# First batch of a fused attention kernel: queries loaded in two halves, and the third key tile pooled by TensorE

## The chip, the cores and the metric

The kernel runs on one core of a Trainium2 chip. The metric is device time in microseconds of one execution; the number compared is the median of several executions. A profile of one more execution comes with it: it gives a span (first to last instruction) and, for every engine, what ran when. The engines are TensorE (PE; its weight loads are listed apart as PEld), VectorE (DVE), ScalarE (ACT), GpSimd (POOL) and SyncE (SP), which here only issues transfers. Every engine runs its instructions in the order in which they were written; they meet by semaphores.

## The reference

Two stages follow each other, for a batch of 4, with 12288 queries of 128 channels each and 384 x 32 key pixels of 128 channels:

```python
r = 4
kv_pool = kv.reshape(B, H // r, r, W // r, r, C).mean(axis=(2, 4))
kv_flat = kv_pool.reshape(B, -1, C) @ w_sr
k = v = kv_flat
s = scale * (q @ k.transpose(0, 2, 1))      # softmax over 768 keys
a = np.exp(s - s.max(-1, keepdims=True)); a /= a.sum(-1, keepdims=True) + 1e-09
x = a @ v
# mixture of adapters: 8 experts of rank 16, the two largest logits of x @ w_gate per token
logits = x @ w_gate
out = x + sum over the two experts e of w[e] * ((x @ A[e]) @ B[e])
```

The part that matters here is the first line: every key is the mean of a 4 x 4 block of pixels, that is, a sum over four rows and four columns (the 1/16 is put into w_sr).

## The kernel before, in words

The keys of a batch come in three tiles (NT = 3) of 256 pooled keys. A tile is held as [128, 4, 2, 512] fp32: 128 partitions, the four pixel rows d, two halves u, and four columns of 128 channels. Each row d is one transfer of 512 KB (load_row, L87). The queries are worked through in 96 chunks of 512; a chunk needs three sets of scores, scores(c, r), one for each key tile r: two products into one of two score banks in PSUM (L318) and one exponential on ScalarE (L319) out of it. Two calls of weigh(c, h) then multiply by the values (L330), twelve products each: h = 0 takes the first three blocks of 128 keys, h = 1 the other three. After that come the adapters.

From chunk 2 on, a software loop (for c in range(2, NCH - 1)) interleaves the scores of later chunks with weigh, normalising and the adapters of earlier ones, and GpSimd pools the keys of the next batch. Before it stands the opening, written out by hand, which this change is about.

Opening, transfers. SP issues the rows of tile 0, then 1 MB of queries (chunks 0 to 3, q0, L125), then tiles 1 and 2, then the next queries (L129, L102). Transfers land in about that order.

Opening, VectorE. For each of the three tiles it adds rows 1, 2 and 3 to row 0 (sum_row, L185), and then folds four columns to two and two to one (sum_cols, L189 and L190).

Opening, TensorE and ScalarE. warm() multiplies constants and has no result that is used. tile_keys(t) turns the pooled tile by a product with the identity in transposing mode (L226); its result is copied to kp_keep by ScalarE (L229), for tile 2 by VectorE (L231); w_sr is applied (k_ps, L234) and copied to the keys kfT (L236, or L238 on VectorE). tile_values(t) makes the values of the same tile (v_ps, L244) and copies them to vext. queries(k, bank) turns chunk k's 512 queries (four products, L582) and ScalarE copies them to qT (L585). The order on TensorE is

```python
tile_keys(0, lambda: queries(0, x_bank())); queries(1, x_bank())
scores(0, 0); tile_values(0); queries(2, x_bank())
scores(1, 0); queries(3, x_bank()); scores(2, 0); scores(3, 0)
warm(6); tile_keys(1); warm(2); scores(0, 1); tile_values(1); scores(1, 1)
weigh(0, 0)
tile_keys(2, during)      # during: cast_half(0); scores(2, 1)
cast_half(1); turn_q(2); turn_q(3)
scores(3, 1); scores(0, 2); tile_values(2); scores(1, 2)
weigh(0, 1); next_scores(); normalise(0)
```

cast_half (VectorE, L607) and cast_q (GpSimd, L107) make fp16 copies of later queries; turn_q (SP, L117) is a transposing transfer of them.

Of the kernel before, what the change touches and what calls it, by code (L numbers as in the profile page):

```python
# [10 lines left out]
FP32 = mybir.dt.float32  # L11
# [10 lines left out]
def kernel(  # L22
# [10 lines left out]
    nc = tc.nc  # L33
    P = 128
    B, N, C = q.tensor.shape
# [5 lines left out]
    NTOK = 512  # L41
    NS = NTOK // P
# [16 lines left out]
    ps_t = ctx.enter_context(tc.tile_pool(name="ps_t", bufs=1, space=bass.MemoryType.PSUM))  # L59
    ps_h = ctx.enter_context(tc.tile_pool(name="ps_h", bufs=1, space=bass.MemoryType.PSUM))  # L60
    x_banks = ExitStack()
    ps_x = x_banks.enter_context(tc.tile_pool(
        name="ps_x", bufs=1, side="right", space=bass.MemoryType.PSUM))
# [5 lines left out]
    def mtile(shape, dtype=FP32, name="hd"):  # L69
        return ps_h.tile(shape, dtype, tag="hd", name=name)  # L70

    mm = nc.tensor.matmul
    g_h = qdram.tile([NCH // 2, E, NS, P, 2], F16, name="g_h")
    qflat = q.rearrange("b n c -> (b n) c")
# [5 lines left out]
    kvt = {}  # L80
    NT = NJ // 2
# [7 lines left out]
    def load_kv(b, t):  # L89
        for d in range(4):  # L90
            load_row(b, t, d)

    GROWS = 2048

    HROWS = GROWS // 2
# [19 lines left out]
    def turn_q(i):  # L115
        new_qT(i)
        nc.sync.dma_start(qT[i], q16[i], transpose=True)  # L117

    q01 = kvpool.tile([P, 2, GROWS // NTOK, NS, C], FP32, tag="kvt", name="q01")
    q0, q1 = q01[:, 0], q01[:, 1]  # L120
    for t in range(NT):
        load_kv(0, t)
        if t == 0:

            nc.sync.dma_start(q0, qflat[0:GROWS].rearrange("(k p s) c -> p k s c", p=P, s=NS))  # L125

    def load_half(i):
        q32[i] = q1[:, 2 * i - 4:2 * i - 2].rearrange("p k s c -> p k (s c)")
# [16 lines left out]
    id_f32 = const.tile([P, P], FP32)  # L145
# [25 lines left out]
    kpT, kfT, vext, sqsum = {}, {}, {}, {}  # L171
# [11 lines left out]
    def sum_row(b, t, d, eng):  # L183
        v = kvt[b, t]
        eng.tensor_tensor(v[:, 0], v[:, 0], v[:, d], op=ALU.add)  # L185

    def sum_cols(b, t, eng):
        v = kvt[b, t][:, 0]
        eng.tensor_tensor(v[:, :, 0:2 * C], v[:, :, 0:2 * C], v[:, :, 2 * C:4 * C], op=ALU.add)  # L189
        eng.tensor_tensor(v[:, :, 0:C], v[:, :, 0:C], v[:, :, C:2 * C], op=ALU.add)  # L190

    def stile(name):
        return ps_s.tile([P, 2, NTOK], FP32, tag="sg", name=name)
# [27 lines left out]
    def tile_keys(t, between=lambda: None):  # L221

        k = slice(2 * t * P, 2 * (t + 1) * P)
        kp_ps = ps_t.tile([P, 2 * P], FP32, tag="tp", name="kp_ps")
        for u in range(2):
            mm(kp_ps[:, u * P:(u + 1) * P], kvt[0, t][:, 0, u, 0:C], id_f32, is_transpose=True,  # L226
               start=(u == 0), stop=(u == 1), skip_group_check=True)
        if t < NT - 1:
            nc.scalar.activation(kpT[0][:, k], kp_ps, AF.Copy)  # L229
        else:  # L230
            nc.vector.tensor_copy(kpT[0][:, k], kp_ps)  # L231
        between()
        k_ps = mtile([P, 2 * P], name="k_ps")
        mm(k_ps, w_sr_sb, kpT[0][:, k], start=True, stop=True)  # L234
        if t < NT - 1:
            nc.scalar.activation(kfT[0][:, k], k_ps, AF.Copy)  # L236
        else:
            nc.vector.tensor_copy(kfT[0][:, k], k_ps)  # L238

    def tile_values(t):  # L240
        v_ps = mtile([P, 2, C + E], name="v_ps")
        for g in range(2):
            j = 2 * t + g
            mm(v_ps[:, g], kpT[0][:, j * P:(j + 1) * P], wext, start=(g == 0), stop=(g == 1),  # L244
               skip_group_check=True)
        if t < NT - 1:
            nc.scalar.activation(vext[0][:, 2 * t:2 * t + 2, 0:C + E], v_ps, AF.Copy)
        else:
            nc.vector.tensor_copy(vext[0][:, 2 * t:2 * t + 2, 0:C + E], v_ps)
# [42 lines left out]
    def prep(c):  # L292
        for b, t, d in loads.get(c, ()):
            load_row(b, t, d)
        for b, t, d in sums.get(c, ()):
            sum_row(b, t, d, nc.gpsimd)
            if d == 3:
                sum_cols(b, t, nc.gpsimd)
# [11 lines left out]
    def scores(c, r):  # L310
        b = c // CPB
        if r == 0:
            tt[c] = ttpool.tile([P, NJ, NTOK], F16, tag="tt", name="tt")
        qc = qT[c // 2][:, c % 2 * NS:(c % 2 + 1) * NS].rearrange("p s t -> p (s t)")
        sg = stile("sg")
        for k in range(2):
            j = 2 * r + k
            mm(sg[:, k], kfT[b][:, j * P:(j + 1) * P], qc, start=True, stop=True)  # L318
        nc.scalar.activation(tt[c][:, 2 * r:2 * r + 2], sg, AF.Exp, bias=0.0, scale=scale)  # L319

    def weigh(c, h, banks=None):
        b = c // CPB
        if banks is not None:
            xps[c] = banks
        elif h == 0:
            xps[c] = ps_x.tile([P, 2, 512], FP32, tag="x", name="xps")
        for j in range(h * NH, (h + 1) * NH):
            for s in range(NS):
                o = xps[c][:, s // 2, (s % 2) * VW:(s % 2 + 1) * VW]
                mm(o, tt[c][:, j, s * P:(s + 1) * P], vext[b][:, j, 0:VW],  # L330
                   start=(j == 0 and s % 2 == 0), stop=(j == NJ - 1 and s % 2 == 1),
                   skip_group_check=True)
# [246 lines left out]
    def queries(k, t):  # L579

        for i in range(NS):
            mm(t[:, i * P:(i + 1) * P], q0[:, k, i], id_f32, is_transpose=True,  # L582
               start=(i == 0), stop=(i == NS - 1), skip_group_check=True)
        qt = qT[k // 2][:, k % 2 * NS:(k % 2 + 1) * NS].rearrange("p s t -> p (s t)")
        nc.scalar.activation(qt, t, AF.Copy)  # L585

    def x_bank():
        return ps_x.tile([P, NTOK], FP32, tag="x", name="q_ps")

    def t_bank():  # L590
        return ps_t.tile([P, NTOK], FP32, tag="tp", name="t_ps")
# [1 line left out]
    def warm(count):  # L593

        t = mtile([P, NS, P], name="w_ps")
        for i in range(count):
            mm(t, id_bf, id_bf.unsqueeze(1).broadcast_to([P, NS, P]), start=True, stop=True)
# [8 lines left out]
    def cast_half(k):  # L606
        nc.vector.tensor_copy(q16[2][:, k * NTOK:(k + 1) * NTOK], q32[2][:, k])  # L607

    for t in range(NT):
        for d in range(1, 4):  # L610
            sum_row(0, t, d, nc.vector)
        sum_cols(0, t, nc.vector)
        if t == 0:
            nc.vector.tensor_copy(a_bf.rearrange("p (r e) -> p e r", e=E),
                                  a_f.rearrange("p (e r) -> p e r", e=E))
            nc.vector.tensor_scalar(b_half, b_f, 0.5, None, op0=ALU.mult)
            nc.vector.tensor_copy(b_bf, b_half)
# [3 lines left out]
    def next_scores():  # L621
        if todo:
            scores(*todo.pop(0))

    tile_keys(0, lambda: queries(0, x_bank()))
    queries(1, x_bank())
    scores(0, 0)
    tile_values(0)
    queries(2, x_bank())
    scores(1, 0)  # L630
    queries(3, x_bank())
    scores(2, 0)
    scores(3, 0)
    warm(6)
    tile_keys(1)
    warm(2)
    scores(0, 1)
    tile_values(1)
    scores(1, 1)
    weigh(0, 0)  # L640

    def during():
        cast_half(0)
        scores(2, 1)

    tile_keys(2, during)
    cast_half(1)
    turn_q(2)
    turn_q(3)
    scores(3, 1)  # L650
    scores(0, 2)
    tile_values(2)
    scores(1, 2)
# [21 lines left out]
    for c in range(2, NCH - 1):  # L675
        b, k = divmod(c, CPB)
# [67 lines left out]
        name="ps_e", bufs=1, reuse_waits="tile", space=bass.MemoryType.PSUM))  # L744
# [65 lines left out]
    def tops4(c, top, y):  # L810
# [20 lines left out]
        name="ps_f", bufs=1, side="right", space=bass.MemoryType.PSUM))  # L831
# [73 lines left out]
    with tc.If(bad_v != 0):  # L905
# [11 lines left out]
        with tc.For_i(0, B) as b:  # L917
            nc.sync.dma_start(kp, kp_all[bass.ds(b, 1)].rearrange("o p k -> p (o k)"))
            for h in range(2):
                s = slice(h * NKV // 2, (h + 1) * NKV // 2)  # L920
# [3 lines left out]
            for h in range(2):  # L924
                v_ps = mtile([P, NJ // 2, C + E], name="gv_ps")
                for g in range(NJ // 2):
                    j = h * NJ // 2 + g
                    mm(v_ps[:, g], kp[:, j * P:(j + 1) * P], wext,
                       start=(g == 0), stop=(g == NJ // 2 - 1))
                nc.vector.tensor_copy(v32[:, h * NJ // 2:(h + 1) * NJ // 2], v_ps)  # L930
            with tc.For_i(0, N, P) as t:
# [3 lines left out]
                q_ps = mtile([P, P], name="gq_ps")  # L935
# [4 lines left out]
                for h in range(2):  # L940
                    mm(s_ps[:, h, 0:NKV // 2], qTf, k32[:, h * NKV // 2:(h + 1) * NKV // 2],
                       start=True, stop=True)
# [9 lines left out]
                for h in range(2):  # L952
                    e_ps = mtile([P, NJ // 2, P], name="ge_ps")
                    for g in range(NJ // 2):
                        j = h * NJ // 2 + g
                        mm(e_ps[:, g], e[:, j * P:(j + 1) * P], id_f32, is_transpose=True,
                           start=(g == 0), stop=(g == NJ // 2 - 1))
# [4 lines left out]
                x = g_w[:, 2, 0:C + E]  # L962
# [63 lines left out]
```

## Time and profile before

| | us |
|---|---|
| median of 3 runs | 379.06 (378.99, 381.55, 379.06) |
| the profiled execution | 378.6 |
| its span | 376.8 |
| TensorE busy | 359.5 |
| ScalarE busy | 310.1 |
| VectorE busy | 300.4 |
| GpSimd busy | 225.1 |

In rows of the timeline and of the chain, the first two numbers are the start and the duration in us from the start of the span; a group of instructions (x8) has the time from its first start to its last end. What stands in square brackets is how long the engine was idle before it, and what ended the wait. A row of the table by stretches gives the stretch and its length, then for PE, PEld, DVE, ACT and POOL the busy time and the number of instructions, then the granted clock of TensorE, the share of the transfer engines and GB/s. A fp32 product that is not a transposing one appears as two matmul rows.

### The profile page before, as it was taken

The numbers are of one execution on the slowest core, as the hardware profiler recorded it, in microseconds if no ns is written. First come the engines' busy times: TensorE is split into PE (matmuls) and PEld (weight loads), VectorE is DVE, ScalarE is ACT, GpSimd is POOL, SyncE is SP. The second block draws the span as 40 slices with busy tenths as digits, with TensorE's granted clock in tenths as the row PEclk, the third lists the DMA queues.
The fourth block names the chain that finished last, engine by engine and source line by source line (L and its number), as shares of the span: only waits on it lengthen the run. The fifth ranks groups of instructions, "written<-read, shape, count | busy, mean of one in ns | idle before, by whom it ended". The sixth has DMA issues, their size and how long they took to land.

```text
span 376.8 us, 10584 instructions
## 1 busy us (share of the span) xinstructions
PE 359.5 (95%) x3943; PEld 265.0 (70%) x3943; DVE 300.4 (80%) x950; ACT 310.1 (82%) x391; POOL 225.1 (60%) x375
## 2 busy tenths in 40 slices
PE   4889999999999999999999999999999999999983
PEld 1446767777777677777777777777776767776772
DVE  3784557888888788788888888888888898889983
ACT  1569999898898898988988898898888888888752
POOL 1013799979699887755679687755434234242244
PEclk9999999999999999999999999999999999999998
DMA  8998999999999999999999999998788699654325
GB/s 260 402 363 202 307 295 331 319 285 303 286 341 318 273 293 328 232 312 317 301 294 370 289 313 308 234 305 262 235 221 259 201 257 242 184 141 142 115 85 198
DMA packets 95593, 101.00 MB, mean 268 GB/s; under 512 B 58804, under 2 KB 59060, under 8 KB 95540
## 3 DMA queue, kind: packets, MB, share of 16 engines
q1 hardware_dynamic: 94068, 100.11, 94.5%
q8 instruction: 31, 0.51, 0.6%
q10 hardware_dynamic: 1472, 0.20, 0.3%
q14 instruction: 22, 0.18, 0.2%
HBM read 62.33 MB, written 25.90 MB: 234 GB/s over the span
## 4 chain that ended last, share of the span: by engine, by line
PE 78%; DVE 7%; POOL 7%; DMA 4%; issue 1%; ACT 1%; ACTq 0%; SPq 0%; POOLq 0%; DVEq 0%
PE xps L330 32%; PE sg L318 28%; PE d_ps L478 5%; PE t_ps L397 5%; PE h_ps L432 4%; DMA b_f<-in_moe_B_dram 3%; POOL kvt L185 2%; DMA kvt<-in_kv_dram 2%; DVE xn L341 2%; DVE ht L435 1%; PE v_ps L209 1%; DVE kvt L185 1%; POOL q L107 1%; POOL kvt L189 1%; PE kp_ps L201 1%
## 5 line engine op out<-in xcount | busy, mean ns | idle before, releaser
L319 ACT ACTIVATE tt<-sg 128x1024 f16<-128x1024 f32 x288 | 277.6, 1022 | 37.9 <-PE sg L318 37.0
L318 PE MATMUL sg<-qT,kfT 128*128 128x512 f16 x576 | 170.1, 379 | 0.4 <-ACT qT L585 0.3
L330 PEld LDWEIGHTS <-tt 128*128 128x128 f16 x2304 | 147.7, 98 | 28.5 <-DVE xn L341 18.6
L330 PE MATMUL xps<-vext,tt 128*128 128x137 f16 x2256 | 166.5, 223 | 0.3 <-DVE xn L341 0.2
L492 DVE TENSOR_TENSOR osb<-d_ps,xn 128x512 f32<-128x512 f32 x85 | 58.7, 691 | 30.0 <-PE d_ps L478 29.7
L357 POOL TENSOR_TENSOR arg<-xn,top 128x64 f32<-128x64 f32 x47 | 14.7, 313 | 102.0 <-DVE top L348 86.2
L341 DVE TENSOR_TENSOR xn<-xps,rinv_all 128x548 f32<-128x548 f32 x94 | 68.4, 728 | 3.3
L318 PEld LDWEIGHTS <-kfT 128*128 128x128 f16 x576 | 49.2, 98 | 24.1 <-issue 0.6
L185 POOL TENSOR_TENSOR kvt<-kvt 128x1024 f32<-128x1024 f32 x27 | 63.6, 2357 | 2.6 <-PE sg L318 2.5
L107 POOL CAST q<-q 128x1024 f16<-128x1024 f32 x45 | 46.8, 1041 | 24.8 <-DMA q<-in_q_dram 24.6
L435 DVE SCALAR_TENSOR_TENSOR ht<-ge,h_ps 128x512 bf16<-128x512 f16 x87 | 58.5, 672 | 1.5 <-PE sg L318 1.0
L478 PEld LDWEIGHTS <-ht 128*128 128x128 bf16 x368 | 27.3, 97 | 24.9 <-DVE ht L435 4.5
L348 DVE MAX8 top<-xn 128x8 f32<-128x8 f32 x376 | 35.1, 156 | 6.2
L408 DVE COPY xt<-t_ps 128x512 bf16<-128x512 bf16 x92 | 36.7, 399 | 0.0
L397 PE MATMUL t_ps<-id_bf,xn 128*128 128x128 bf16 x376 | 36.3, 219 | 0.0
L478 PE MATMUL d_ps<-b_bf,ht 128*128 128x128 bf16 x340 | 32.9, 219 | 1.0 <-DVE ht L435 0.9
L432 PE MATMUL h_ps<-xt,a_bf 128*128 128x512 bf16 x87 | 33.0, 379 | 0.1
L337 DVE RECIPROCAL rinv_all<-xps 128x4 f32<-128x4 f32 x94 | 17.1, 182 | 14.6 <-PE xps L330 12.3
L397 PEld LDWEIGHTS <-xn 128*128 128x128 bf16 x376 | 25.9, 98 | 0.3
L360 POOL TENSOR_SCALAR msk<-msk 128x64 f32<-128x64 f32 x47 | 20.1, 428 | 4.1
L361 POOL TENSOR_TENSOR arg<-arg,msk 128x64 f32<-128x64 f32 x47 | 15.0, 319 | 3.9
L359 POOL TENSOR_TENSOR arg<-arg,msk 128x64 f32<-128x64 f32 x47 | 15.0, 319 | 3.7
(147 smaller groups left out, 220.8 us busy)
## 6 DMA issues: line engine op xcount, KB each, us to landing
kvt<-in_kv_dram SPq DMA_DIRECT2D x48, 512.0 KB
q<-in_q_dram SPq DMA_DIRECT2D x46, 512.0 KB
out_dram<-osb SPq DMA_DIRECT2D x44, 512.0 KB
ge<-g_h SPq DMA_DIRECT2D x45, 256.0 KB
out_dram<-osb SPq DMA_DIRECT2D x8, 256.0 KB
q<-in_q_dram SPq DMA_DIRECT2D x1, 1024.0 KB
qT<-q SPq DMA_TRANSPOSE x46
g_h<-g_sb SPq DMA_DIRECT2D x45, 16.0 KB
```

The source lines that it names most:

```text
L107: nc.gpsimd.tensor_copy(q16[i], q32[i].rearrange("p k n -> p (k n)"))
L185: eng.tensor_tensor(v[:, 0], v[:, 0], v[:, d], op=ALU.add)
L318: mm(sg[:, k], kfT[b][:, j * P:(j + 1) * P], qc, start=True, stop=True)
L319: nc.scalar.activation(tt[c][:, 2 * r:2 * r + 2], sg, AF.Exp, bias=0.0, scale=scale)
L330: mm(o, tt[c][:, j, s * P:(s + 1) * P], vext[b][:, j, 0:VW], start=(j == 0 and s % 2 == 0), stop=(j == NJ - 1 and s % 2 == 1), skip_group_ ...
L341: nc.vector.tensor_tensor(xn[c].rearrange("p (b s) v -> p b s v", b=2), xv, ri.rearrange("p (b s) -> p b s", b=2).unsqueeze(3).broadcast_t ...
L397: mm(columns(t_ps, c, s), src[:, s], id_bf, is_transpose=True, start=(s == 0), stop=(s == NS - 1), skip_group_check=True)
L408: nc.vector.tensor_copy(to, t_ps)
L432: mm(h_ps, a_bf, xT[c], start=True, stop=True)
L435: nc.vector.scalar_tensor_tensor(hgT[c].rearrange("p (k a) t -> p k (a t)", k=2), gE[c // 2][:, h:h + NS // 2].rearrange("p a t k -> p k ( ...
L478: mm(dps[c][:, s], columns(hgT[c], c, s), b_bf, start=(s == 0 and fresh), stop=(s == NS - 1), skip_group_check=True)
L492: nc.vector.tensor_tensor(osb[:, lo:hi], d, xn[c][:, lo:hi, 0:C], op=ALU.add)
```

## The change

The 1 MB of queries becomes two transfers of 512 KB: chunks 0 and 1 behind tile 0, chunks 2 and 3 behind tile 1. In tile 2 VectorE no longer adds rows; it folds the columns of rows 1, 2 and 3, each by itself. TensorE adds the rows: turn_row(d, u) multiplies by the identity, now as ordinary fp32 products, and accumulates all rows in PSUM. Row 0 is not folded at all; its four columns are four products. So there are fourteen such products in place of two transposing ones. They use the second half of a two-bank tile x_all, whose first half holds the queries being turned. queries(2) and queries(3), weigh(0, 0), scores(2, 1) and scores(3, 1) change places, and the warm-up products after the first 18 go from eight to four.

```diff
-        if t == 0:
-
-            nc.sync.dma_start(q0, qflat[0:GROWS].rearrange("(k p s) c -> p k s c", p=P, s=NS))
+        if t < 2:
+            nc.sync.dma_start(
+                q0[:, 2 * t:2 * t + 2], qflat[t * HROWS:(t + 1) * HROWS].rearrange(
+                    "(k p s) c -> p k s c", p=P, s=NS))
...
-    def sum_cols(b, t, eng):
-        v = kvt[b, t][:, 0]
+    def sum_cols(b, t, eng, d=0):
+        v = kvt[b, t][:, d]
...
-            nc.vector.tensor_copy(kpT[0][:, k], kp_ps)
+            nc.vector.tensor_copy(kpT[0][:, k], x_all[:, 1, 0:2 * P])
...
+    x_all = ps_x.tile([P, 2, NTOK], FP32, tag="x", name="q_ps")
+
+    def turn_row(d, u):
+        for f in range(4 if d == 0 else 1):
+            mm(x_all[:, 1, u * P:(u + 1) * P], kvt[0, NT - 1][:, d, u, f * C:(f + 1) * C], id_f32,
+               start=(d == 0 and u == 0 and f == 0), stop=(d == 3 and u == 1),
+               skip_group_check=True)
...
         for d in range(1, 4):
-            sum_row(0, t, d, nc.vector)
-        sum_cols(0, t, nc.vector)
+            if t < NT - 1:
+                sum_row(0, t, d, nc.vector)
+            else:
+                sum_cols(0, t, nc.vector, d)
+        if t < NT - 1:
+            sum_cols(0, t, nc.vector)
...
+    xq = x_all[:, 0]
+    tile_keys(0, lambda: queries(0, xq))
+    queries(1, xq)
     scores(0, 0)
     tile_values(0)
-    queries(2, x_bank())
     scores(1, 0)
-    queries(3, x_bank())
+    warm(4)
+    queries(2, xq)
     scores(2, 0)
+    tile_keys(1, lambda: turn_row(0, 0))
+    queries(3, xq)
+    turn_row(0, 1)
     scores(3, 0)
-    warm(6)
-    tile_keys(1)
-    warm(2)
     scores(0, 1)
     tile_values(1)
     scores(1, 1)
-    weigh(0, 0)
+    for u in range(2):
+        turn_row(1, u)
+    scores(2, 1)
+    for d in (2, 3):
+        for u in range(2):
+            turn_row(d, u)
 
     def during():
         cast_half(0)
-        scores(2, 1)
+        scores(3, 1)
 
     tile_keys(2, during)
     cast_half(1)
     turn_q(2)
     turn_q(3)
-    scores(3, 1)
+    weigh(0, 0)
     scores(0, 2)
```

More of the change, by code (lines that the diff above doesn't have):

```diff
@@ L223, in tile_keys @@
         k = slice(2 * t * P, 2 * (t + 1) * P)
[L224 to L227, printed above, removed]
         if t < NT - 1:
+            kp_ps = ps_t.tile([P, 2 * P], FP32, tag="tp", name="kp_ps")
+            for u in range(2):
+                mm(kp_ps[:, u * P:(u + 1) * P], kvt[0, t][:, 0, u, 0:C], id_f32, is_transpose=True,
+                   start=(u == 0), stop=(u == 1), skip_group_check=True)
             nc.scalar.activation(kpT[0][:, k], kp_ps, AF.Copy)
         else:
-            nc.vector.tensor_copy(kpT[0][:, k], kp_ps)
+            nc.vector.tensor_copy(kpT[0][:, k], x_all[:, 1, 0:2 * P])
         between()
@@ L585, in queries @@
         nc.scalar.activation(qt, t, AF.Copy)
-    def x_bank():
-        return ps_x.tile([P, NTOK], FP32, tag="x", name="q_ps")
+    x_all = ps_x.tile([P, 2, NTOK], FP32, tag="x", name="q_ps")
[4 more added lines that the diff above has]
+               skip_group_check=True)
     def t_bank():
@@ L623, in next_scores @@
             scores(*todo.pop(0))
-    tile_keys(0, lambda: queries(0, x_bank()))
-    queries(1, x_bank())
+    xq = x_all[:, 0]
+    tile_keys(0, lambda: queries(0, xq))
+    queries(1, xq)
     scores(0, 0)
     tile_values(0)
-    queries(2, x_bank())
     scores(1, 0)
-    queries(3, x_bank())
+    warm(4)
+    queries(2, xq)
     scores(2, 0)
+    tile_keys(1, lambda: turn_row(0, 0))
+    queries(3, xq)
+    turn_row(0, 1)
     scores(3, 0)
-    warm(6)
-    tile_keys(1)
-    warm(2)
     scores(0, 1)
@@ L639 @@
     scores(1, 1)
-    weigh(0, 0)
+    for u in range(2):
+        turn_row(1, u)
+    scores(2, 1)
+    for d in (2, 3):
+        for u in range(2):
+            turn_row(d, u)
     def during():
         cast_half(0)
-        scores(2, 1)
+        scores(3, 1)
     tile_keys(2, during)
```

## The prediction

> **What bounds the kernel now.** I read the page first, then the table by stretches, the PE's waits, and only then the opening in the timeline and in the chain that ended last.
>
> ```profile
> PE 359.5 (95%) x3943; PEld 265.0 (70%) x3943; DVE 300.4 (80%) x950; ACT 310.1 (82%) x391; POOL 225.1 (60%) x375
> ...
> 12.00:20.00 8.00, 6.72 (x38) 4.06 (x38) 5.49 (x9) 6.70 (x11) 0.00 (x0) 1.00 1.03 409
> 20.00:26.00 6.00, 4.81 (x32) 2.80 (x30) 5.14 (x7) 3.19 (x6) 0.00 (x0) 1.00 1.03 393
> ...
> 80.00:120.00 40.00, 40.00 (x463) 30.62 (x461) 33.48 (x108) 35.62 (x45) 33.24 (x49) 1.00 1.09 298
> ...
> PE d_ps L478 <- DVE ht L435: 0.8, 1, 0.8
> PE kp_ps L201 <- POOL kvt L190: 0.5, 2, 0.3
> PE xps L330 <- DVE xn L341: 0.2, 1, 0.2
> ```
>
> The reader is to see that from 30 to 340 us TensorE waits 0.8 + 0.5 + 0.2 = 1.5 us in all (the last three rows), and is busy 40.00 of 40.00 us in a stretch of the loop. So the loop neither takes nor gives back much: whatever moves the moment at which it starts moves the end by about as much. The change touches only what stands before 30 us, so the whole question is that moment. I take as its mark the resumption of weigh(0, 1), which waits for the last exponential of chunk 0. Here is the chain into it, and the VectorE and transfer rows of the stage:
>
> ```profile
> 24.17 0.70 DVE kvt L189
> 24.89 0.43 DVE kvt L190
> ...
> 25.38 0.45 PE kp_ps L226 x2
> 25.85 0.43 DVE kp_keep L231
> 26.33 0.70 PE k_ps L234 x2
> 27.03 0.45 PE sg L318 x2
> 27.50 1.95 ACT tt L319 x2
> 29.44 0.05 issue
> 29.49 0.67 PE xps L330 x8
> ...
> 32.51 0.72 PE xps L330 x12
> ...
> 15.23 3.78 DVE L185 TENSOR_TENSOR kvt<-kvt 128x1024 f32<-128x1024 f32 x3 [2.30 <-DMA kvt<-in_kv_dram]
> ...
> 20.35 3.78 DVE L185 TENSOR_TENSOR kvt<-kvt 128x1024 f32<-128x1024 f32 x3 [0.15 <-DMA kvt<-in_kv_dram]
> ...
> 3.45 0.65 SPq L125 DMA_DIRECT2D q<-in_q_dram  x1
> 5.00 10.21 SPq L87 DMA_DIRECT2D kvt<-in_kv_dram  x8
> ```
>
> Before, the mark is at 29.49. VectorE's adds of tile 2 (L185, L189, L190) end at 24.89 + 0.43, about 25.33, and lead to it.
>
> **Landings.** The first add of tile 1 starts when its second row has landed, at 15.23, and the same add of tile 2 at 20.35: four rows of 512 KB in 5.12 us, 1.28 us each, while the table by stretches shows 409 and 393 GB/s. In the changed order queries 0 and 1 (512 KB) lie ahead of tile 1 and queries 2 and 3 between tiles 1 and 2. Tile 1 therefore lands one such step earlier (adds from 13.95; with the 3.78 of L185 and 1.16 of the column adds, done at 18.9 instead of 20.2). Tile 2 has the same bytes ahead of it and lands as before: its rows 1, 2, 3 at 20.31, 21.59, 22.87, and so queries 2 and 3 land two steps ahead of its row 1, at 20.31 - 2.56 = 17.75. The one issue more on SP's queue costs about 0.65 us there (the row at 3.45), and the queue has it free: its eight row issues from 5.00 stretch over 10.21 us, where eight of 0.65 are 5.2.
>
> **What the change takes from VectorE.** In tile 2 the three adds of whole rows go, and each of rows 1 to 3 gets the pair L189, L190 (24.17 to 25.33, 1.16 us) as it lands: 20.35, 21.63, 22.91, the last done at 24.07. A last product of 256 columns (0.70 us, the row k_ps) would put the copy to kp_keep at 24.07 + 0.04 + 0.70 + 0.04 = 24.85, where it was at 25.85. That is 1.0 us gained, if TensorE is there by then. I find that it is not.
>
> **What it moves.** Before, the queries were all turned and copied by 18.4 us:
>
> ```profile
> 16.33 0.62 ACT L585 ACTIVATE qT<-q_ps 128x512 f16<-128x512 f32 x1
> ...
> 17.71 0.65 ACT L585 ACTIVATE qT<-q_ps 128x512 f16<-128x512 f32 x1
> 18.19 2.00 ACT L319 ACTIVATE tt<-sg 128x1024 f16<-128x1024 f32 x2
> 20.73 0.38 ACT L229 ACTIVATE kp_keep<-kp_ps 128x256 f32<-128x256 f32 x1 [0.54 <-PE kp_ps L226]
> 21.90 0.38 ACT L236 ACTIVATE kfT<-k_ps 128x256 f16<-128x256 f32 x1 [0.79 <-PE k_ps L234]
> 23.40 1.02 ACT L319 ACTIVATE tt<-sg 128x1024 f16<-128x1024 f32 x1 [1.11 <-PE sg L318]
> ...
> 27.50 2.85 ACT L319 ACTIVATE tt<-sg 128x1024 f16<-128x1024 f32 x3 [0.19 <-PE sg L318]
> ...
> 14.89 0.63 PE L244 MATMUL v_ps<-wext,kp_keep 128*128 128x136 f32 x4
> 15.36 0.61 PE L582 MATMUL q_ps<-id_f,q 128*128 128x128 f32 x4
> 15.80 0.59 PE L318 MATMUL sg<-qT,kfT 128*128 128x512 f16 x2
> ...
> 17.01 0.66 PE L582 MATMUL q_ps<-id_f,q 128*128 128x128 f32 x4 [0.61 <-ACT qT L585]
> ...
> 21.16 0.70 PE L234 MATMUL k_ps<-kp_keep,w_sr_sb 128*128 128x256 f32 x2 [0.47 <-ACT kp_keep L229]
> ...
> 22.77 0.59 PE L318 MATMUL sg<-qT,kfT 128*128 128x512 f16 x2
> 22.98 0.64 PEld L244 LDWEIGHTS v_ps<-wext,kp_keep 128*128 128x128 f32 x4
> 23.20 0.63 PE L244 MATMUL v_ps<-wext,kp_keep 128*128 128x136 f32 x4
> ...
> 26.86 1.29 PE L318 MATMUL sg<-qT,kfT 128*128 128x512 f16 x4
> ```
>
> Durations from these rows: queries to the start of their copy 17.71 - 17.01 = 0.70, the copy 0.62; scores 23.20 - 22.77 = 0.43 of TensorE, and 23.40 - 22.77 = 0.63 to their exponential; exponentials one after another (2.85 - 1.02) / 2 = 0.92, and 1.02 until a reader may go; k_ps to the kfT copy 21.90 - 21.16 = 0.74, and 26.86 - 26.33 = 0.53 of TensorE; twelve products of weigh 0.72; 0.05 for each hand-over. The fp32 product of 128 columns by the identity does not occur. Its nearest row is v_ps: two products of 136 columns take 15.36 - 14.89 = 0.47, so 0.24 each. Its weight loads, four in 0.64 with all but the last hidden, could set 0.32. I take 0.25; four are 1.0 us.
>
> Now the new order. Queries 2 at 17.80 (landing), copy 18.50 to 19.12; scores(2, 0) at 19.17; exponential at 19.80. ScalarE's next instruction, the kp_keep copy of tile 1, is queued behind that exponential: 20.72 to 21.10, although tile 1 was ready at 18.9. k_ps 21.15, its copy 21.89. Queries 3 run behind k_ps (0.53), at 21.68; their copy 22.38 to 23.00. The second half of row 0 waits for that copy: both use the one tile x_all, and the changed instruction list has a ScalarE wait there. It runs 23.05 to 24.05 and, queued behind it, scores(3, 0) 24.05, exponential 24.68, then that of (0, 1) 25.60 to 26.62. There are two score banks, so scores(2, 1), two sets after (0, 1), waits for this: 26.67 to 27.10. Rows 2 and 3 of tile 2 are queued behind it: 27.10 to 28.10, with VectorE done since 24.07. The copy to kp_keep starts at 28.31 instead of 25.85. From there: k_ps 28.78, kfT copy 29.52, weigh(0, 0), now behind k_ps, 29.31 to 30.03, scores(0, 2) 30.03, exponential 30.66 to 31.68, mark **31.72**, against 29.49: 2.2 us later.
>
> After the mark the work is the same. SP's transposing transfers of queries wait, as before, for cast_half(1), which follows the kfT copy: that copy starts at 29.52 instead of the 26.33 + 0.74 = 27.07 of before, and all that is queued behind on SP (the next loads of queries and kv) moves with it, by about 2.4 us, while its readers on TensorE move by 2.2; the 0.2 is within the range. Warm-up products fall from 8 to 4, at places where TensorE waits anyway; GpSimd's casts wait for loads whose place among the bytes is unchanged.
>
> ```profile
> 6.13 5.75 PE L597 MATMUL w_ps<-id_bf 128*128 128x512 bf16 x18 [0.26 <-DVE vext L180]
> ...
> 9.07 0.15 PEld L597 LDWEIGHTS <-id_bf 128*128 128x128 bf16 x1 [0.28 <-issue]
> 9.50 1.89 PEld L597 LDWEIGHTS <-id_bf 128*128 128x128 bf16 x9 [0.28 <-issue]
> ```
>
> The warm-up products start at 6.13; up to 9.50 one stands 0.43 us behind the other (9.07, 9.50), and the last nine weight loads take 1.89, 0.21 each: TensorE starts at half rate. The longest hole that my schedule gives it, between queries 2 or 3 and what follows their copy, is 0.92 us, and the old order had one of 0.61 us (the row at 17.01) with normal products behind it. So I add nothing for the rate. The Trainium skill, "TensorE: Matmul & The Clock Gate" (section "What's actually happening"), says that the clock falls to half after an idle window of about 3.4 us; by that page the holes here are too short, and the sum stays.
>
> **Sum.** The profiled execution took 378.6 us, its span of 376.8 and 1.8 around it; with 2.2 it would be 380.8. It lies 0.46 below the median of the runs, 379.06, so the forecast is 379.06 + 2.2 = 381.3. A measurement of this kernel tells about 1%, 3.8 us, from no change; the forecast is within it.
>
> **Rivals.** *VectorE's chain sets the end after all* (the other side: faster). The copy comes at 24.85, 1.0 us earlier than before, and the time is 378.1. It decides by TensorE reaching the last two products by 24.1, where I have 27.6. For it: VectorE and the chain before lead exactly there. Against it: queries 2 and 3 would have to land 3.5 us earlier than the 1.28 us per row allow. 0.13.
>
> *The delay is partly given back.* If POOL's and VectorE's chains in the loop do not move with the mark, the 1.5 us of waits from 30 to 340 us shrink: 2.2 - 1.5 = 0.7, 379.8. Against it: these chains start from the casts and transfers behind the mark. 0.12.
>
> *The fp32 products are dearer.* Eight of them lie on the path (four before scores(3, 0), four before the copy). At four times a turning product, (15.80 - 15.36) / 4 = 0.11, they take 0.44, 0.19 more each: 1.5 more, 382.8. The v_ps row speaks against it. The Trainium skill, "TensorE: Matmul & The Clock Gate" (section "Terms"), says that the transposing mode is 4 times as fast for fp32; by that page's ratio the time would be this one, while the trace's 0.24 against 0.11 is nearer 2. 0.08.
>
> *TensorE falls to half rate* in the holes of 18 to 25 us. It was slow from 6.13 to 9.50 above, 3.4 us; such a stretch costs half of itself, 1.7 more: 383.0. 0.07.
>
> **How the numbers follow.** The forecast has 0.60. The range leaves out the faster rival (0.13) and the half rate (0.07): from 379.0, below the give-back, to 382.9, above the dear products; the weight-load end of the product, 0.32, adds 8 x 0.07 = 0.6 and lies within. Over 1% slower (382.85): half rate, and a few of the dear-product cases, 0.10. Over 1% faster: 0.01.
>
> **What would show it.** In the changed trace: queries 2 start near 17.8 with a wait for their transfer; VectorE's last add of tile 2 ends near 24.1; ScalarE waits little from 18.5 on; TensorE's last row-3 product starts after 27, behind scores(2, 1) released by ScalarE; the kp_keep copy on VectorE near 28.3; the mark near 31.7. I am wrong if queries 2 start well before 17, if the row-0 products do not wait for the copy of queries 3, or if the loop between the mark and the end is shorter than before.

## The result: 1.5% slower, more than forecast

The changed kernel takes 385.22 us in the median of four runs (382.23 to 387.49), the kernel before 379.02; the ratio is 1.0149 (95% interval 1.0108 to 1.019). Here and below the ratio is an estimate from all the runs, not the quotient of the two medians, which would be 1.0164. Forecast was 381.3, within 379.0 to 382.9. The sign was right, the size too small by 4 us and outside the range. TensorE's granted clock, as a mean over a run, is 0.987 to 0.992 in the four runs; it is 0.994 to 0.998 in 35 of the 36 runs of the kernel before that were taken beside the experiments.

The profiled execution of the changed kernel took 385.41 us with a span of 383.4, that is 6.8 and 6.6 more than the one before. First the page, the table by stretches, and TensorE's waits from 37 us, behind the mark, to 340 us. Lines of the changed kernel are one higher (L319 is the scores, L331 weigh), L583 turns queries, L594 is turn_row, L586 the copy of queries.

```profile
PE 363.3 (95%) x3964; PEld 269.5 (70%) x3965; DVE 299.0 (78%) x951; ACT 310.5 (81%) x391; POOL 225.4 (59%) x375
...
12.00:20.00 8.00, 4.58 (x24) 2.59 (x24) 5.25 (x9) 4.08 (x7) 0.00 (x0) 0.97 0.92 309
20.00:26.00 6.00, 5.10 (x19) 4.06 (x20) 3.85 (x7) 1.90 (x3) 0.00 (x0) 0.50 1.01 400
...
80.00:120.00 40.00, 40.00 (x460) 30.58 (x458) 33.55 (x108) 35.41 (x45) 33.19 (x49) 1.00 1.12 298
...
PE kp_ps L202 <- POOL kvt L191: 0.7, 2, 0.4
PE d_ps L479 <- DVE ht L436: 0.4, 1, 0.4
PE xps L331 <- DVE xn L342: 0.2, 1, 0.2
```

The loop is as it was: 40.00 of 40.00 us busy, 1.3 us of waits where there were 1.5. In the opening TensorE is less busy, and two other columns that were level before have changed: from 12 to 20 us the transfers move 309 GB/s instead of 409, and from 20 to 26 TensorE's granted clock is 0.50 instead of 1.00. Next, the chain into the mark (weigh(0, 1) resumes), the weight loads that resume there, and three rows of TensorE for the price of the fp32 products:

```profile
2.21 10.86 DMA b_f<-in_moe_B_dram
...
13.08 0.54 SPq L87
...
13.66 6.51 DMA q<-in_q_dram
...
20.22 1.13 PE q_ps L583 x4
...
26.68 0.61 ACT qT L586
...
27.33 1.16 PE q_ps L594 x8
28.49 0.45 PE sg L319 x2
...
28.96 1.03 ACT tt L320
...
31.54 0.91 PE q_ps L594 x8
...
32.54 0.44 DVE kp_keep L232
...
35.98 0.47 PEld L331 LDWEIGHTS <-tt 128*128 128x128 f16 x8 [0.16 <-ACT tt L320]
...
28.33 1.03 PE L319 MATMUL sg<-qT,kfT 128*128 128x512 f16 x4
...
31.38 1.05 PE L594 MATMUL q_ps<-id_f,kvt 128*128 128x128 f32 x8
...
32.27 0.59 PE L319 MATMUL sg<-qT,kfT 128*128 128x512 f16 x2
```

VectorE's adds no longer stand in this chain. It begins with the landing of a small load for the adapters, b_f, for which SP has waited; SP then issues a row of tile 1 at 13.08 and the second query load at 13.66; that load lands 6.5 us later; then come the queries, their copy, the products of row 0 behind that copy, scores, an exponential, the last products, and the kp_keep copy at 32.54 where it was at 25.85. The mark is at 35.98 instead of 29.49, 6.5 us later, and the span 6.6 longer.

### The profile page after: what moved, and what is told of

The parts are those of the page before. It is cut to its first block, busy times and chain, and to the rows that moved or that the text cites. A ratio compares the mean times of both kernels' runs of the same rounds, so it can differ in the third digit from the quotient of the medians.

```text
span 383.4 us, 10629 instructions
## 1 busy us (share of the span) xinstructions
PE 363.3 (95%) x3964; PEld 269.5 (70%) x3965; DVE 299.0 (78%) x951; ACT 310.5 (81%) x391; POOL 225.4 (59%) x375
## 4 chain that ended last, share of the span: by engine, by line
PE 76%; DMA 8%; POOL 6%; DVE 5%; issue 1%; ACT 1%; ACTq 0%; SPq 0%; POOLq 0%; DVEq 0%
PE xps L331 30%; PE sg L319 26%; PE d_ps L479 5%; PE t_ps L398 4%; PE h_ps L433 4%; DMA b_f<-in_moe_B_dram 3%; POOL kvt L186 2%; DMA kvt<-in_kv_dram 2%; DMA q<-in_q_dram 2%; DVE xn L342 2%; DMA ge<-g_h 1%; DVE ht L436 1%; PE q_ps L594 1%; PE v_ps L210 1%; POOL q L107 1%
## 5 line engine op out<-in xcount | busy, mean ns | idle before, releaser
L319 PE MATMUL sg<-qT,kfT 128*128 128x512 f16 x576 | 170.3, 380 | 1.0 <-ACT qT L586 0.7
L331 PEld LDWEIGHTS <-tt 128*128 128x128 f16 x2304 | 147.7, 98 | 28.2 <-DVE xn L342 18.7
L331 PE MATMUL xps<-vext,tt 128*128 128x137 f16 x2256 | 166.3, 223 | 0.2 <-DVE xn L342 0.2
L358 POOL TENSOR_TENSOR arg<-xn,top 128x64 f32<-128x64 f32 x47 | 14.8, 315 | 105.5 <-DVE top L349 89.8
L319 PEld LDWEIGHTS <-kfT 128*128 128x128 f16 x576 | 49.2, 98 | 24.0 <-issue 1.4
```

Of the source, the lines that this page charges most:

```text
L331: mm(o, tt[c][:, j, s * P:(s + 1) * P], vext[b][:, j, 0:VW], start=(j == 0 and s % 2 == 0), stop=(j == NJ - 1 and s % 2 == 1), skip_group_ ...
```

## The experiments

Five theories were tried. **A**: the second query load is late because SP's issues stall behind the landing of the two small adapter loads a_f and b_f, and the transfers run dry. **C** and **F**: TensorE's hole ahead of that load puts it at half rate, and that costs the rest; **F** adds that no whole idle stretch of 3.4 us is needed. **D**: the wait inside x_all lies on the path. **E**: row sums on TensorE pay if the queries stay early. The mark and the start of queries 2 are given for the profiled execution of each kernel, the times are medians. e1, e3, e4 and e5 were run beside a kernel before of 378.84 us, e2, e6, e7 and e8 beside one of 379.08.

**The stall taken away (e1_small_on_pool).**

```diff
-    nc.scalar.dma_start(a_f, moe_A.rearrange("e c r -> c e r"))
+    nc.gpsimd.dma_start(a_f, moe_A.rearrange("e c r -> c e r"))
-    nc.scalar.dma_start(b_f, moe_B.rearrange("e r c -> r e c"))
+    nc.gpsimd.dma_start(b_f, moe_B.rearrange("e r c -> r e c"))
```

> The changed kernel with the two small adapter loads (a_f, b_f) issued by GpSimd instead of ScalarE, so that no row load on SP waits for their landing. Theory A (SP's queue stalls behind the landing of a_f and b_f, the transfers run dry, queries 2 and 3 land at 20.2 us instead of 17.75): transfers stay near 400 GB/s from 13 to 17 us, queries 2 are turned near 17.8, TensorE keeps the full clock, the mark (weigh(0, 1) resumes) is near 31.7 and the time near 381.2, some 4 below the changed kernel. Rival B (the second query load is late for another reason, its own transfer or the order in the queue): queries 2 still start near 20.2 and the time stays near 385.

Measured: 380.76 us, ratio 1.0063 (1.0042 to 1.0085). First the kernel before, the two issues of SP behind its waits, and then the changed kernel: SP's rows of the timeline around the stall, what SP waited for up to 20 us (total, times, longest), and the stretch from 13 to 17 us:

```profile
11.11 0.54 SPq L87 DMA_DIRECT2D kvt<-in_kv_dram  x1
...
12.09 0.53 SPq L87 DMA_DIRECT2D kvt<-in_kv_dram  x1
...
5.58 0.60 SPq L87 DMA_DIRECT2D kvt<-in_kv_dram  x1
11.58 0.53 SPq L87 DMA_DIRECT2D kvt<-in_kv_dram  x1
13.08 0.54 SPq L87 DMA_DIRECT2D kvt<-in_kv_dram  x1
...
SPq L87 <- DMA a_f<-in_moe_A_dram: 5.4, 1, 5.4
...
SPq L87 <- DMA b_f<-in_moe_B_dram: 1.0, 1, 1.0
...
13.00:17.00 4.00, 3.44 (x22) 2.07 (x19) 2.81 (x4) 3.43 (x7) 0.00 (x0) 1.00 0.81 242
```

And this experiment: SP's rows, the same stretch, queries 2, and the mark:

```profile
4.13 2.65 SPq L87 DMA_DIRECT2D kvt<-in_kv_dram  x4
6.83 0.60 SPq L124 DMA_DIRECT2D q<-in_q_dram  x1
...
13.00:17.00 4.00, 3.44 (x21) 2.08 (x19) 3.06 (x6) 3.42 (x7) 0.00 (x0) 1.00 1.03 402
...
17.99 0.66 PE L583 MATMUL q_ps<-id_f,q 128*128 128x128 f32 x4 [0.17 <-DMA q<-in_q_dram]
...
31.78 0.47 PEld L331 LDWEIGHTS <-tt 128*128 128x128 f16 x8 [0.16 <-ACT tt L320]
```

In the changed kernel SP issues nothing from 6.2 to 11.58, waiting for a_f, issues one row and waits for b_f until 13.08, and the transfers fall to 242 GB/s. Why an issue on SP is made to wait for a load that ScalarE issued, these profiles do not show. With the small loads elsewhere the second query load is issued at 6.83 instead of 13.66, the rate stays at 402, queries 2 start at 17.99 (forecast 17.80) and the mark comes at 31.78 (forecast 31.72). Theory A holds, and what is left, 380.76 us, is near the forecast of 381.3.

**The split undone (e4_one_load).** The changed kernel with one query load of 1 MB behind tile 0.

```diff
-        if t < 2:
-            nc.sync.dma_start(
-                q0[:, 2 * t:2 * t + 2], qflat[t * HROWS:(t + 1) * HROWS].rearrange(
-                    "(k p s) c -> p k s c", p=P, s=NS))
+        if t == 0:
+            nc.sync.dma_start(q0, qflat[0:GROWS].rearrange("(k p s) c -> p k s c", p=P, s=NS))
```

> The changed kernel with the queries in one load of 1 MB behind tile 0, as before; everything else as changed. Theory A with the order: the loads run as in the kernel before (b_f near 12.1, no dry stretch), queries 2 start right behind the 4 warm-up products near 17.4, full clock, mark near 31.3, time near 380.8: the new order on TensorE and ScalarE alone costs 1.8. Rival (the order costs nothing and the split everything): mark at or before 29.5, time 378 to 379. Rival (the split costs nothing): 385.

Measured: 381.67 us, ratio 1.0099 (1.0065 to 1.0133). SP's rows, the stretch, and the mark (line numbers are two lower here):

```profile
4.87 9.62 SPq L87 DMA_DIRECT2D kvt<-in_kv_dram  x8
...
13.00:17.00 4.00, 3.44 (x21) 2.06 (x19) 1.77 (x3) 3.54 (x7) 0.00 (x0) 1.00 1.03 410
...
31.93 0.47 PEld L329 LDWEIGHTS <-tt 128*128 128x128 f16 x8 [0.16 <-ACT tt L318]
```

SP still waits for the small loads (eight issues take 9.62 us), but the rate stays at 410 GB/s: half a megabyte more was in flight. So the stall itself is old; the split took its cover away. The mark is 0.6 later than expected: tile 1 lands later in this order, and TensorE waits 0.97 us for it at 20.39, which the expectation left out. Full clock, landings as before, and still 2.4 us late: that is the new order on TensorE and ScalarE.

**The split alone (e5_split_alone).** The kernel before with only its query load split as in the changed kernel (the diff of e4, the other way round).

> The kernel before with the split load alone, all else as before. Theory A: the transfers run dry between 13 and 17 us as in the changed kernel, queries 2 wait until 20 and all behind them on TensorE with them; the hole is over 4 us, the clock falls to half, the mark comes near 35.5 and the time near 385. Rival (in the old order the split is harmless): below 380.

Measured: 382.51 us, ratio 1.0091 (1.0059 to 1.0124). The two stretches, queries 2, the mark:

```profile
13.00:17.00 4.00, 3.40 (x20) 2.09 (x18) 3.12 (x6) 2.83 (x6) 0.00 (x0) 1.00 0.89 276
...
20.00:26.00 6.00, 5.50 (x18) 2.83 (x19) 4.04 (x6) 3.87 (x5) 0.00 (x0) 0.52 1.03 406
...
20.50 1.09 PE L583 MATMUL q_ps<-id_f,q 128*128 128x128 f32 x4 [4.07 <-DMA q<-in_q_dram]
...
35.36 0.47 PEld L331 LDWEIGHTS <-tt 128*128 128x128 f16 x8 [0.27 <-ACT tt L320]
```

The mechanism is as expected (276 GB/s, a hole of 4.07 us, half rate, mark 35.36), the time 2.5 us less than expected: this execution's mark is 5.9 us late and its time, 383.2, only 4.6. 1.3 us came back behind the mark. The shortest of the four runs, 381.09 us, had a mean clock of 0.996, so the clock hardly fell there; the others had 0.986 to 0.991.

**More warm-up (e3_warm16).**

```diff
-    warm(4)
+    warm(16)
```

> The changed kernel with 16 warm-up products instead of 4 ahead of queries 2, so that TensorE is busy while it waits for the second query load. Theory C (the hole of 2.4 us drops TensorE's clock to half for two stretches of 3.4 us, and that costs the 1.8 us that the late landing does not explain): the granted clock is 1.00 from 20 to 26 us, queries 2 still start near 20.2, the mark is near 34.1 instead of 35.98, the time near 383.4. Rival (the clock does not lie on the path, ScalarE and the transfers do): clock 1.00 but the mark within 0.5 us of 36 and the time near 385.

Measured: 384.37 us, ratio 1.0149 (1.0132 to 1.0166), so the same ratio as the changed kernel. VectorE's first use of a_f, SP, the warm-up products, the clock, queries 2, and the mark:

```profile
14.77 0.46 DVE L626 CAST a_bf<-a_f 128x128 bf16<-128x128 f32 x1 [1.88 <-DMA a_f<-in_moe_A_dram]
...
14.76 1.18 SPq L87 DMA_DIRECT2D kvt<-in_kv_dram  x2
...
17.06 3.61 PE L605 MATMUL w_ps<-id_bf 128*128 128x512 bf16 x16 [0.52 <-ACT vext L248]
...
20.00:26.00 6.00, 3.50 (x17) 2.29 (x15) 3.12 (x5) 1.72 (x3) 0.00 (x0) 0.78 1.02 389
...
22.49 0.66 PE L583 MATMUL q_ps<-id_f,q 128*128 128x128 f32 x4 [1.81 <-DMA q<-in_q_dram]
...
37.14 0.47 PEld L331 LDWEIGHTS <-tt 128*128 128x128 f16 x8 [0.16 <-ACT tt L320]
```

In this execution a_f landed only at 14.76, and SP and VectorE went on in the same moment. So queries 2 came at 22.49, 2.3 us later again, a hole of 1.81 us was left, and the clock fell after all. On theory C this profiled execution says nothing. It says that the landing of a_f moves by some 3 us from one execution to another, which would also give the changed kernel its spread of 5 us; that was not shown.

The other four runs do bear on theory C: their mean clock is 0.995 to 0.998, as in the kernel before, and they still took 383.91 to 384.62 us. An estimate from the rows: the warm-up products end at 17.06 + 3.61 = 20.67, queries 2 cannot start earlier, and with the 13.79 us that e1 took from there the mark is at 34.46, 5.0 late, which gives 383.8. So at full clock the late load and the new order are still paid, and the changed kernel, with its lower clock, takes about 1 us more (385.22). No profile of these four runs was kept, so where their queries 2 started is not known.

**A hole without a late load (e8_pool_no_warm).** e1 without its `warm(4)`.

> The kernel of e1 without the four warm-up products ahead of queries 2: a hole of about 1.8 us from 16.1 to 18 us, with the landings as in e1. Theory F (a stretch of 3.4 us with TensorE busy for well under half of it is enough for half rate, no whole idle stretch is needed): the granted clock falls to 0.5 for at least 3.4 us between 17 and 26, and the mark comes 0.8 or more after 31.77. Rival (only an idle stretch of 3.4 us does it, and the drop in the changed kernel came from its longer hole): clock 1.00 throughout, mark within 0.3 of 31.77.

Measured: 381.28 us, ratio 1.0063 (1.0035 to 1.0092), not to be told from e1. The three runs took 382.86, 381.28 and 380.68 us with mean clocks of 0.993, 0.996 and 0.997; the first is the profiled one. Its single us of the table by stretches, queries 2, and the mark:

```profile
19.00:20.00 1.00, 0.32 (x3) 0.11 (x2) 0.51 (x2) 0.60 (x1) 0.00 (x0) 1.00 1.02 406
20.00:21.00 1.00, 1.00 (x7) 0.92 (x6) 0.03 (x1) 0.60 (x1) 0.00 (x0) 0.71 1.02 406
21.00:22.00 1.00, 1.00 (x7) 1.00 (x6) 0.97 (x2) 0.70 (x2) 0.00 (x0) 0.50 1.04 414
22.00:23.00 1.00, 1.00 (x5) 0.71 (x5) 0.84 (x3) 0.00 (x0) 0.00 (x0) 0.50 1.00 381
23.00:24.00 1.00, 1.00 (x5) 0.63 (x3) 0.87 (x2) 0.38 (x1) 0.00 (x0) 0.58 1.06 391
...
18.43 0.66 PE L583 MATMUL q_ps<-id_f,q 128*128 128x128 f32 x4 [1.72 <-DMA q<-in_q_dram]
...
33.33 0.47 PEld L331 LDWEIGHTS <-tt 128*128 128x128 f16 x8 [0.16 <-ACT tt L320]
```

A hole of 1.72 us, with one of 0.69 us behind it, was followed by half rate from about 20.4 to 23.8, after TensorE was already busy again. Its mark is 1.55 later than e1's, 0.44 of it from the later landing. So in the profiled execution theory F holds. In the other two runs the clock stayed at e1's (0.994 to 0.996), and they were 1.6 and 2.2 us shorter: this kernel brings the half rate in some executions and not in others, and the median does not show its price. From the start of queries 2 to the mark, the same work took 13.79 us at full rate (e1), 14.65 and 14.90 with one stretch of half rate (e3, e8), 15.76 with two (the changed kernel, 20.22 to 35.98).

**The wait inside x_all (e6_pool_q3_own_bank).** On top of e1:

```diff
-    queries(3, xq)
+    queries(3, t_bank())
```

> The kernel of e1 with queries 3 turned in the bank of the other turning products instead of in x_all, so that the second half of row 0 need not wait for ScalarE's copy of queries 3. Theory D (that wait lies on the path): the products of row 0 fill the hole of 0.7 us, scores(3, 0) start near 23.2 instead of 24.13, the mark comes near 30.85 instead of 31.77 and the time 0.9 below e1. Rival (ScalarE's exponentials set the pace of that stage anyway): mark and time as e1.

Measured: 380.72 us, ratio 1.0038 (1.0018 to 1.0058). The second half of row 0, the mark, and the loop's waits from 32 to 340 us:

```profile
22.38 1.06 PE L594 MATMUL q_ps<-id_f,kvt 128*128 128x128 f32 x8
...
30.92 0.47 PEld L331 LDWEIGHTS <-tt 128*128 128x128 f16 x8 [0.16 <-ACT tt L320]
...
PE kp_ps L202 <- POOL kvt L191: 1.3, 2, 1.1
```

At the mark theory D is right: row 0 runs in the hole, and the mark is 0.86 earlier than e1's. The time is not shown to follow: the ratio is 0.25% lower, but the intervals overlap, and above the kernel before run beside each the medians are 1.64 us (e6) and 1.92 us (e1). In the profiled execution the loop then waits 1.3 us for GpSimd's sums, where e1 has no such wait.

**The small loads moved in the kernel before (e2_before_small_on_pool).** The diff of e1 on the kernel before.

> The kernel before with the two small adapter loads issued by GpSimd instead of ScalarE. Theory A says that the old order had enough bytes in flight (1 MB of queries ahead of tile 1) to cover SP's wait for a_f and b_f, so the transfers never ran dry and nothing is gained: the mark stays within 0.4 us of 29.5 and the time within 0.2% of the kernel before. If the wait cost the old order too, it is faster by over 0.3%.

Measured: 379.32 us, ratio 1.0009 (0.9995 to 1.0023): nothing gained, as theory A says. Its profiled mark is 30.12, 0.2 later than the bound of the expectation; that execution's tile 1 was done 0.6 us later than in the kernel before.

**Row sums on TensorE, queries early (e7_rows_queries_early).** One load as in e4, and this order (new and moved lines marked):

```diff
+    queries(2, xq)
     scores(1, 0)
+    queries(3, xq)
+    scores(2, 0)
+    scores(3, 0)
+    warm(2); turn_row(0, 0)
+    tile_keys(1, lambda: turn_row(0, 1))
+    turn_row(1, 0); turn_row(1, 1)
+    scores(0, 1); tile_values(1)
+    turn_row(2, 0); turn_row(2, 1)
+    scores(1, 1)
+    turn_row(3, 0); turn_row(3, 1)
     tile_keys(2, during)      # during: cast_half(0); scores(2, 1)
     cast_half(1); turn_q(2); turn_q(3)
+    scores(3, 1); scores(0, 2); tile_values(2); weigh(0, 0)
     scores(1, 2)
```

> The summing of tile 2's rows on TensorE without the moved queries: one load of 1 MB behind tile 0 and queries 0 to 3 turned early, as before; row 0 is multiplied where the warm-up products stood, rows 1 to 3 as VectorE finishes them, weigh(0, 0) behind the values of tile 2. Theory E (the idea pays once the queries stay early, and the order was what cost): VectorE's adds of tile 2 end near 24.1, the kp_keep copy starts near 25.2 instead of 25.85, the mark is near 28.8 instead of 29.49, the time 0.6 below the kernel before (0.17%). Rival (the 14 products cost TensorE what VectorE saves): mark at 29.5 or later, time at or above the kernel before.

Measured: 378.59 us against 379.08, ratio 0.9975 (0.9953 to 0.9996): just faster than the kernel before, and the fastest of all. The medians alone are 0.13% apart. The copy to kp_keep, weigh(0, 1), and the first reader of its result:

```profile
25.51 0.42 DVE L230 COPY kp_keep<-q_ps 128x256 f32<-128x256 f32 x1 [0.99 <-PE q_ps L592]
...
29.32 0.88 PE L329 MATMUL xps<-vext,tt 128*128 128x137 f16 x12
...
30.25 0.18 DVE L336 RECIPROCAL rinv_all<-xps 128x4 f32<-128x4 f32 x1 [1.43 <-PE xps L329]
```

The copy starts 0.34 earlier than before, not 0.65 as expected. weigh(0, 1) runs in one piece here, so there is no resumption to compare; its end is no earlier than before (30.25 where it was 30.18), which speaks for the rival. So theory E rests on the runs alone: their gain, 0.25%, is of the size expected, with an interval that nearly reaches none, and where it is made is not shown.

## Why the prediction was wrong

- **That the new order costs 2.2 us**: right. From queries 2 to the mark the forecast had 13.92 us, e1 took 13.79; its mark was late by 31.78 - 29.49 = 2.3. The steps between agree too: scores(3, 0) at 24.13 for 24.05, the kp_keep copy at 28.34 for 28.31. So this is no luck of the sum.
- **The fp32 product at 0.25**: right. Four take 28.33 - 27.33 = 1.00 behind a wait (the scores behind row 0 start at 28.33), 0.89 in 31.38 to 32.27. The dearer price, 0.44, is out.
- **Row 0 waiting for the copy of queries 3**: right, worth 0.86 at the mark (e6). **VectorE done long before the copy**: right; its last add ended 6 us ahead of it.
- **"Tile 2 has the same bytes ahead of it and lands as before"**, and with it queries 2 and 3 at 17.75: wrong by 2.2 to 2.4 us. The step that failed is the sentence on SP's queue. I read eight issues in 10.21 us as spare time for one more. It was two waits, of 4.9 us for a_f and 0.4 us for b_f, and SP's waits in the trace of the kernel before name them. Here the bytes ahead set the landing only while enough were in flight (410 GB/s in e4, 242 in the changed kernel): the split put 512 KB, 1.28 us of transfer, behind those waits, and the waits ended later as well (11.58 and 13.08 instead of 11.11 and 12.09).
- **"So I add nothing for the rate"**: wrong by 2.0 us in the profiled execution. The hole forecast at 0.92 us was 0.69 in e1 and harmless (full clock), but in the changed kernel the late load made another one, of 2.41 us, ahead of queries 2. The half-rate rival had the mechanism, and 1.7 us for one stretch. At the mark one stretch cost less, 14.65 - 13.79 = 0.86 (e3) and 14.90 - 13.79 = 1.11 (e8), but the changed kernel had two, and 15.76 - 13.79 = 1.97. I had treated the rival as independent of the landing, which it is not. By the Trainium skill, "TensorE: Matmul & The Clock Gate" (section "What's actually happening"), it takes an idle window of about 3.4 us; the hole of 1.72 us in e8's profiled execution speaks against that as a rule for holes.
- **The sum**: landing 2.23 (20.22 - 17.99), half rate 1.97 and order 2.29 make the 6.49 of the mark. The span grew by 6.6. These are differences between the changed kernel, e1 and the kernel before, so they add up by themselves; that the 1.97 are the clock's rests on e3 and e8, not on a run of the changed kernel at full clock.
- **"The loop neither takes nor gives back much"**: right here, but only to about 1.3 us: e5's profiled execution got that much back, e6's waited as much for GpSimd's sums.

## What to carry to other kernels

A queue that issues rarely is not a queue with room: look for what each gap in its issues waits for, and count the bytes in flight when it stalls, not the bytes ahead in program order. A load cut in two, with one half moved later, no longer covers the waits that the whole load covered. And where a load may come late, TensorE's hole can have a second price, the half-rate stretch behind it, so the two belong in one rival and not in two.

## What the runs showed of the hardware

TensorE fell to half rate with holes of 1.72 us (e8, the profiled run of three), 1.81 us (e3), 2.41 us (the changed kernel) and 4.07 us (e5), and not with holes of up to 1.17 us (e7, ahead of 12.65 us). In e8 the half rate began near 20.4, 2 us after the hole had ended, and lasted 3.4 us while TensorE was fully busy; in the changed kernel it began near 19.5, inside the hole, and lasted twice as long. In the 3.4 us ahead of it TensorE was busy for 1.2 to 1.4 us in the changed kernel, e3 and e8. That a share of busy time in such a stretch decides, rather than an idle one, fits these executions but was not tried by itself.

In two other kernels the one run with a clearly lower mean clock is also the longest: 383.93 us at 0.989 against 380.54 to 381.74 at 0.996 to 0.998 (e4), and for the kernel before 382.87 at 0.987 against 377.66 to 381.4 at 0.994 to 0.998. What made the clock fall in those two runs is not known, since no profile of them was kept.

The small load a_f (64 KB) was issued by 2.2 us and landed at some time between 11.1 and 14.8 us, depending on the execution (SP went on at 11.11, 11.58 and 14.76), with the row loads of SP beside it. Which of the loads it lost its turns to was not tried.
